# The opening of an attention and gated feed-forward kernel: its hand-written order through the fifth tile's step written anew, with copies as entries of their own, line sums moved to VectorE, and late query loads placed behind the weights

## The chip, the cores and the metric

One Trainium2 chip, one of its cores. The metric is the device time of one execution in microseconds (us). The kernel before takes 1026.68 us, the median of three runs (1026.49 to 1027.34). The profile is of one further execution.

## What is computed

Attention over keys that are 4x4 averages of an image, followed by a gated feed-forward layer, all in one launch.

```python
# q (4, 12288, 128), kv (4, 384, 32, 128), w_sr (128, 128)
kv_pool = kv.reshape(B, H//4, 4, W//4, 4, C).mean(axis=(2, 4))
k = v = kv_pool.reshape(B, -1, C) @ w_sr            # 768 keys per image
a = exp(s - max(s)),  s = (q @ k.T) / sqrt(C)
x = (a / a.sum(-1)) @ v                              # 49152 rows of 128
out = (relu(x @ w_gate) * (x @ w_val)) @ w_out       # d_ff = 1536
```

The kernel does not subtract the maximum and divides by the row sums only at the end, squared, since the gate and the value are both linear in x.

## The kernel before, in words

**Tiles.** The rows are cut into 96 tiles of 512. Per tile TensorE does 6 rows of score matmuls (keys in 6 chunks of 128), 6 value matmuls, and for each of 12 blocks of the hidden layer one value projection, one gate projection and one output projection. Tiles 0 to 3 are the lead: their attention is done with scores transposed (keys on partitions, `scores` and `lead_values`), and their row sums are made on TensorE with a block of ones (`lead_sums`, four tiles side by side in 32-column strips of the array).

**Order.** Every engine runs its instructions in the order in which the program lists them. That order is written out by hand. The string `OPENING` lists the work up to the first gate and value projections of tile 0; after it, the loop over `k` from 4 runs a list of words per step (`FIRST` for steps 4 and 5, then `STEADY`). Step `k` does the scores of tile k (`s0` to `s3`, exponentials `e0` to `e3`), the projections of tile k-3 (`v`, `y`, `g`, `h`) and the output of tile k-4 (`o`, closed by `oT`). Step 4 is the fifth tile's step, step 5 the sixth. `FIRST` begins `r v1 o0 v8 v10 o1 v4 s0`: in step 5, `o0` and `o1` are the output matmuls of tile 1 that read the gate products of hidden blocks 0 and 1.

**Words.** A word names a step and its numbers; `v1.2` is tile 1, hidden block 2, `S0.5` tile 0, key chunk 5.

- `a`, `b`, `c`, `p`, `r`: sums of image lines (128x512 float32), then of pixels, of one key chunk, on the engine that `ENGINES` names (`a` ScalarE, `v` VectorE, `p` GpSimd; VectorE if none). `SUMS` says which lines. A chunk has four lines; those not summed are summed by TensorE while it turns them.
- `T5.3`: TensorE turns line 3 of chunk 5, four 128x128 transposes that add in one bank (`turn_add`); `T3.p` two transposes, of the two pixel sums; `T2.r` one. `kvT` copies the turned chunk out, `pj` multiplies it by `w_sr`, `key` stores it as keys, `vt` and `val` make the values of it.
- `cast`, `qt`, `qT`: queries to 16 bits, turned, copied.
- `S`, `V`, `U`: score matmul, value matmul, sums with ones. `R`: inverts the row sums (VectorE). `xT`: copies a tile's attention result.
- `v`, `g`: value and gate projection; in the old opening each also issues the copy of its result (`keep_value`) or the gate product (`gated`). `y` is that copy, `h` that product (VectorE, reads the gate's bank and the copy).
- `gate`, `W0`, `W1`, `wo`: a one-column copy on GpSimd that waits for an image line, then the loads of the weights, issued by GpSimd. `gate22` waits for line 2 of chunk 5.

**Banks.** PSUM has eight banks of 128x512. `bank` takes the first free one in the order in which they were freed; two of the eight (6 and 7) are given up for a wide tile (`wide_ps`, scores of tiles from 4 on) when the opening ends.

**Loads.** The sync queue (SP) carries the lines of key chunks 0 and 1, then w_sr, queries and lines of chunks 2 and 3, four transfers of lines of chunks 4 and 5 (`kv_line`), each 512 KB, and then eight transfers of 64 KB for the queries of tiles 5 and 4 (`q_late`, line 173). DMA issues of SP and GpSimd wait on their own queues in listed order.

## Time and profile before

| what | us |
|---|---|
| median of three runs | 1026.68 |
| span of the profiled execution, first to last instruction | 1024.5 |
| TensorE busy in it | 1019.4 |
| ScalarE busy | 919.9 |
| VectorE busy | 861.8 |
| GpSimd busy | 524.8 |
| first transpose of an image line on TensorE starts at | 8.07 |
| first value projection (tile 0) starts at | 27.84 |
| step 5 starts at (its first value projection) | 45.71 |
| granted TensorE clock, mean | 1.000 |

Times inside the run are counted from the span's first instruction. The median is 2.2 us above the span of the profiled execution: start and end of an execution lie outside of the span. In a timeline row, the columns are start, duration of the merged stretch, engine, line, operation, what is written and read, shape and count, and in brackets the idle time before it with what ended it. On TensorE a matmul's row shows when it starts and a modelled end; the next one starts before that end.

## The change

The list `OPENING` is written anew and now runs through the whole of step 4: its scores (`s`, `e`), the projections of tile 1, and the output of tile 0 (`o`, `oT`) are mixed with those of tile 0, and the loop starts at step 5. The exponentials (`E`), the copies of value projections (`y`) and the gate products (`h`) are words of their own, each with its place in its engine's order. A word may name its bank after an `@`. Several outputs of one bank may now be added in any order of blocks (`o_left`, `sums_left`). `ENGINES` names VectorE for nearly all line sums (GpSimd keeps `a1`), for more copies of the opening, and for three of the 24 copies `y` of tiles 0 and 1 (1.11, 1.7, 1.9). Chunks 2 and 5 get line sums and a sum of pixels (`a`, `p`, `r`), and give up eight and eight transposes for one each. The ones matmuls go in six groups of four (`U0` to `U5`) in place of one of 20 and one of 4. The gate before the weights waits for line 1 of chunk 4 (`gate2.1`). The loads of the late queries become words (`ql4`, `ql5`) behind `W1`; a one-element memset on GpSimd into their tile goes ahead of them. The queries of tiles 6 and 7 are loaded in four words (`qd`), their transposing transfer (`tq1`) stands after `s0`.

```diff
     ENGINES = dict(word.split(":") for word in """
-        key0:a val0:a a1:p kvT1:a key1:a val1:a key2:a val2:a a3:p b3:p p3:p kvT3:a val3:a
-        cast0:a cast1:a qT1:a cast3:a cast4:p cast5:p xT1:a xT3:a
+        a1:p p1:v kvT1:a cast0:v cast1:v key1:a kvT0:v qT1:v qT0:a val1:v key0:a cast3:v cast2:v
+        val0:v qT3:a a2:v qT2:v p2:v a3:v r2:v b3:v c3:v kvT2:a p3:v key2:a kvT3:a val2:v a5:v
+        key3:v p5:v a4:v r5:v b4:v val3:a c4:v kvT5:a p4:v key5:v kvT4:v val5:a key4:v val4:v
+        cast4:p xT1:v xT2:v cast5:p y1.11:v y1.2:a xT3:v y1.4:a xT0:a y1.0:a y1.3:a y0.6:a y0.4:a
+        y0.5:a y0.3:a y0.11:a y0.1:a y1.8:a y0.0:a y0.8:a y1.7:v y0.2:a y1.10:a y0.9:a y0.7:a
+        y0.10:a y1.1:a y1.5:a y1.9:v y1.6:a
     """.split())
     OPENING = """
-        T0.1 T1.3 cast1 T0.3 cast0 T1.2 T0.2 a1 p1 T1.p T0.0 kvT1 kvT0 pj1 qt1 pj0 T2.0 qT1 a3
...
+        a1 p1 T1.p@0 T0.0@1 T1.3 T1.2 T0.2 kvT1 T0.1 cast0 pj1@0 cast1 T0.3 key1 qt1@2 kvT0 vt1@0
+        qt0@3 qT1 pj0@1 qT0 val1 S1.1@2 key0 S0.1@0 E1.1 vt0@1 S0.0@3 cast3 S1.0@4 E0.1 cast2
+        V1.1@2 qt3@5 E1.0 val0 V0.1@0 qt2@1 qT3 a2 V1.0 E0.0 S3.1@4 qT2 S3.0@5 E3.1 V0.0 p2
+        S2.1@1 E3.0 a3 T2.2@3 V3.1@4 E2.1 r2 V3.0 b3 S2.0@5 T2.r T2.3 E2.0 c3 V2.1@1 kvT2 U1@6
+        V2.0 pj2@3 p3 U0 key2 T3.p@5 S0.2@3 kvT3 vt2@7 S1.2@5 E0.2 val2 gate2.1 a5 pj3@7 W0 E1.2
+        S3.2@3 key3 V0.2 p5 E3.2 S2.2@5 S2.3@7 a4 E2.2 V1.2 W1 ql4 ql5 T5.2@3 E2.3 r5 vt3@5 V2.2
+        b4 T5.r val3 V3.2 T5.3 wo c4 S1.3@5 kvT5 V2.3 E1.3 S0.3@7 p4 pj5@3 E0.3 U2 key5 T4.p@5
+        V1.3 kvT4 vt5@3 S3.5@7 val5 V0.3 E3.5 S2.5@5 pj4@3 E2.5 S1.5@7 key4 V3.5 E1.5 vt4@3
+        S1.4@5 val4 V2.5 E1.4 cast4 S2.4@3 V1.5 E2.4 S3.4@7 qT4 V1.4 S3.3@5 E3.4 xT1 V2.4 S0.5@3
+        E3.3 qd1 V3.4 xT2 S0.4@7 E0.5 cast5 v1.11@2 V3.3 E0.4 y1.11 v1.2@5 qd3 g1.2@1 qT5 y1.2
+        v1.4@3 xT3 qd0 V0.4 V0.5 y1.4 g1.11@2 qd2 h1.2 g1.3@5 xT0 v1.0@4 g1.4@3 h1.11 y1.0 v1.3@1
+        v0.6@0 U3 h1.4 y1.3 v0.4@2 g0.6@4 y0.6 U4 h1.3 v0.5@1 y0.4 v0.3@3 h0.6 g0.4@0 y0.5 v0.1@5
+        v0.11@2 h0.4 y0.3 U5 g0.3@1 g0.5@4 y0.11 R o4@0 v1.8@3 y0.1 o6 h0.5 v0.0@2 y1.8 s0 h0.3
+        g0.1@5 y0.0 g1.8@3 tq1 v1.7@4 h0.1 e0 o3 v0.8@1 v0.2@2 h1.8 g0.8@5 y0.8 s1 y1.7 y0.2
+        g0.9@3 g0.2@1 o1 e1 h0.8 g0.11@2 v1.10@4 h0.2 o5 y1.10 v0.9@5 s2 h0.11 qn11 y0.9 o2
+        g0.0@1 e2 v0.10@4 v0.7@2 h0.9 g1.10@5 o8 y0.7 o11 h0.0 v1.1@3 y0.10 s3 h1.10 g0.10@1 y1.1
+        v1.5@2 g0.7@4 h0.10 e3 o0 v1.6@3 h0.7 v1.9@5 g1.7@1 y1.5 o10 y1.9 o9 y1.6 o7 g1.0@2 h1.7
+        g1.1@4 g1.9@3 g1.6@5 oT g1.5@1 h1.0 h1.9 h1.5 h1.6 h1.1
     """.split()
...
-    SUMS = [{}, {"a": [0, 1]}, {}, {"a": [0, 1], "b": ["s", 2], "c": ["s", 3]}, {"a": [0, 1], "b": ["s", 2], "c": ["s", 3]}, {}]
+    SUMS = [{}, {"a": [1, 0]}, {"a": [0, 1]}, {"a": [0, 1], "b": ["s", 2], "c": ["s", 3]}, {"a": [0, 1], "b": ["s", 2], "c": ["s", 3]}, {"a": [0, 1]}]
...
     def q_load_tile(i):
         q32 = work.tile([128, T], FP32, tag="o_t", bufs=2, name="q32_late")
+        nc.gpsimd.memset(q32[0:1, 0:1], 0.0)
...
     def lead_sums(chunks):
-        if "sums" not in x_banks:
-            x_banks["sums"] = bank([128, T])
         for jc in chunks:
+            first = "sums" not in x_banks
+            if first:
+                x_banks["sums"] = bank([128, T])
+            sums_left[0] -= 1
...
-    q_load_tile(5)
-    q_load_tile(4)
...
         elif head == "U":
-            lead_sums(range(at[0] * (NJC - 1), NJC - 1 + at[0]))
+            lead_sums(at)
...
         elif head == "v":
             value_proj(*at)
+        elif head == "y":
             keep_value(*at)
         elif head == "g":
             gate_proj(*at)
+        elif head == "h":
             gated(*at)
...
         elif head == "gate":
-            nc.gpsimd.tensor_copy(gate, line(at[0] // 4, at[0] % 4)[:, 0, 0:1])
+            nc.gpsimd.tensor_copy(gate, line(2 * at[0], at[1])[:, 0, 0:1])
+        elif head == "ql":
+            q_load_tile(at[0])
...
+        elif head == "o":
+            out_proj(0, at[0])
+            image_step(1, 0, at[0])
+        elif head == "oT":
+            out_moves.extend(out_turn(0))
+        elif head == "s":
...
+            score_block(LEAD, at[0])
+        elif head == "e":
+            exp_block(LEAD, at[0])
+            if at[0] % 2:
+                a_turn(LEAD, at[0] - 1, at[0] + 1)
...
-    for k in range(LEAD, last + 1):
+    for k in range(LEAD + 1, last + 1):
```

## What was predicted, before the result was known

> **What bounds the kernel now.** First the page's busy times, then the chain of waits, then TensorE's timeline around the change.

> ```profile
> PE 1019.4 (100%) x5048; PEld 489.5 (48%) x5048; DVE 861.8 (84%) x1432; ACT 919.9 (90%) x1931; POOL 524.8 (51%) x1308
> ...
> PE 98%; DMA 1%; ACT 1%; SPq 0%; issue 0%
> ```

> TensorE is busy throughout and the chain stays on it for 98%. From step 5 on its 512-column matmuls start 0.216 us apart, so the change can only alter when step 5 gets going. That is read from the opening.

> ```profile
> 22.27 0.66 PE L270 MATMUL bank_ps<-ident,kv_line 128*128 128x128 f32 x4
> ...
> 27.84 0.38 PE L455 MATMUL bank_ps<-xT,wv 128*128 128x512 f16 x1
> 28.06 0.38 PE L468 MATMUL bank_ps<-xT,wg 128*128 128x512 f16 x1
> 28.37 1.26 PE L432 MATMUL bank_ps<-aT,ones 128*32 128x512 f16 x20
> 29.56 0.39 PE L455 MATMUL bank_ps<-xT,wv 128*128 128x512 f16 x1
> ...
> 45.71 0.38 PE L455 MATMUL bank_ps<-xT,wv 128*128 128x512 f16 x1
> 45.93 0.38 PE L496 MATMUL bank_ps<-hT,wo 128*128 128x512 f16 x1
> 46.14 0.59 PE L455 MATMUL bank_ps<-xT,wv 128*128 128x512 f16 x2
> 46.57 0.38 PE L496 MATMUL bank_ps<-hT,wo 128*128 128x512 f16 x1
> ```

> T5.3, the last image line, starts at 22.27 (the weight load before it waited for the DMA). Step 5 begins at 45.71 and its second output matmul, o1 of tile 1, at 46.57: the point I compare. VectorE, which makes the gate products that this matmul reads:

> ```profile
> 29.23 0.69 DVE L476 SCALAR_TENSOR_TENSOR hT<-bank_ps,val 128x512 f16<-128x512 f32 x1
> 30.36 0.72 DVE L440 STREAM_TRANSPOSE sums_turned<-bank_ps 128x512 f32<-128x512 f32 x1 [0.44 <-PE bank_ps L432]
> ...
> 31.49 6.69 DVE L476 SCALAR_TENSOR_TENSOR hT<-bank_ps,val 128x512 f16<-128x512 f32 x11
> 38.65 0.69 DVE L462 CAST val<-bank_ps 128x512 f16<-128x512 f32 x1 [0.47 <-PE bank_ps L455]
> 39.26 7.42 DVE L476 SCALAR_TENSOR_TENSOR hT<-bank_ps,val 128x512 f16<-128x512 f32 x12
> 46.59 0.71 DVE L504 STREAM_TRANSPOSE o_t<-bank_ps 128x512 f32<-128x512 f32 x1
> ```

> From 29.23 to 47.30 VectorE has hardly a gap. TensorE is the bound on paper, but in this stretch VectorE runs level with it.

> **Part 1: TensorE's own work.** Turning line by line costs 0.11 us per transpose (four from 18.69 to the next matmul at 19.13). Chunks 2 and 5 fall from 16 transposes to nine each: 14 x 0.11 = -1.5. The ones matmuls use 32-column strips, and each switch to or from them costs time: 28.06 to 28.37 is 0.31 instead of 0.216, the way out 0.11 (29.88 to 30.21 for four that take 0.216). That is 0.2 per group; six groups instead of two add 0.8. [...]

> The new list has 48 transposes (5.3), 6 projections (1.3), 22 turns of queries and values (16 x 0.056 and 6 x 0.056: 1.2), 108 matmuls of 512 columns (23.3), 6 groups of ones (2.5) and 4 score pairs (0.324 each, 1.3): 34.9 us. It begins with T1.p, for which a1 on GpSimd (6.37 to 7.63) and p1 on VectorE (7.66 to 8.09) are needed: 8.25. Without a wait, step 5 would begin at 43.2 instead of 45.71.

> **Part 2: the line that lands last.** T5.3 cannot go before 22.27 (a little earlier perhaps, below). Behind it the list holds 83 matmuls of 512 columns (17.9), four groups of ones (1.7), the score pairs (1.3) and small ones (1.2): 22.1 us. So step 5 begins at 44.4 at the earliest, 1.3 ahead of before. Moving sums off TensorE buys nothing ahead of this line: TensorE then waits for it.

> **Part 3: sums and copies moved.** On VectorE a line sum takes 0.69, a pixel sum 0.42 (GpSimd's took 1.26 and 0.73). VectorE gains four of the larger kind (a2, a3, b3, a5), three pixel sums (p2, p3, p5) and two half ones (r2, r5): 4 x 0.69 + 3 x 0.42 + 2 x 0.25 = 4.5, before 23 us, and it was busy 4.5 of the 14 us from 8 to 22: hidden, unless T2.r or T5.r stand in front of TensorE; uncovered it would cost up to 4.5. T5.r needs a5, p5, r5 behind val2, key3 and a4 in VectorE's queue; lines 0 and 1 of that pair are there by 19.3 (the gate on line 2 fired at 20.60, pieces of 512 KB follow each other by 1.3: 12.89 to 14.21 in the first waits), so 19.8 + 0.69 + 0.3 + 0.4 + 0.69 + 0.25 = 22.1. It comes level with T5.3. I take T5.3 at 22.4 (22.2 to 22.6).

> **Part 4: ScalarE up to the first gate product.** Behind T5.3 the list has 11 of the 24 exponentials, paced 0.48 apart (the row of eight from 24.83 takes 4.05). The first follows T5.3 (0.44) and S1.3's 0.41: 23.25. Without waits the eleven and val5 (0.22) end at 28.8. Two waits: val5 stands ahead of E3.5 and needs vt5, which comes behind U2, T4.p and V1.3 on TensorE, at 24.7 (ScalarE idle 0.6); S1.5 is told to use bank 7, which E3.5 frees (0.2). So y1.2, queued behind E0.4, runs 29.6 to 30.2, and h1.2, the first product, starts at 30.2, where before it was 29.23. xT3 is put ahead of it on VectorE and ends at the same time. Bounds: 29.4 (no wait), 30.6 (T5.3 at 22.6, and a little in each hand-over).

> **Part 5: VectorE to the end of its list.** From h1.2 to the end of h1.1: 24 products at 0.60 (11 in 6.69), R 1.13 (30.36 to 31.49), y1.7 and y1.9 at 0.61, oT 0.7, the last one's tail 0.08: 17.5. Before, the same stretch had 24 products, R and one copy (16.1), and ended at 46.59 after 1.2 us of gaps. I take 1.0 of gaps (0.1 to 1.3): 30.2 + 17.5 + 1.0 = 48.7. **That is the step that decides:** the list ends `oT g1.5 h1.0 h1.9 h1.5 h1.6 h1.1`, and step 5 begins `v1 o0 v8 v10 o1`. o1 reads h1.1, now the last of all, with oT and four products ahead of it. Even if TensorE reached g1.5 on time, five products take 3.1 us from there, while o1 is due 1.1 us after it. The banks say the same: at g1.5 five of six hold gates that wait for VectorE. So o1 runs at 48.7 where it ran at 46.57: +2.1. Behind it waits all of step 5 on TensorE. VectorE and ScalarE catch up during the wait, so I expect nothing more to be late; the 0.27 at 55.3 (a score pair that waited for ScalarE) may go.

> **Part 6: loads.** The gate fires on line 1 of chunk 4, 1.3 earlier, at 19.3. The weights were there in time before (27.84 waited for none), so this is worth nothing on the path. The late queries are no longer issued from 12.89 on, but behind GpSimd's four weight issues (0.7, 0.6, 0.6, 0.6), from 21.9; eight at 0.31 end at 24.4. The median landing of `q_late` was 5.9 us, so tile 4's are there by 28 to 29; its cast (0.61) and transposing transfer (5.4) give 34 to 35. s0 comes at 35.9: some 1 us of cover. On GpSimd `wo`, both casts and the `qd` loads stand behind the memset, on SP qT4, qT5, tq1 and the first image lines behind the late queries; all have several us. Cost nothing; if the landing slips by 2 us, s0 waits 1.

> **Sum.** Own work and line: up to -1.3. VectorE's end, which replaces it: +2.1 (from 29.4 + 17.5 + 0.1 = 47.0, +0.4, to 30.6 + 17.5 + 1.3 = 49.4, +2.8). The span 1024.5 becomes 1026.6; the median stood 2.2 above the span: **1028.8**.

> **Rivals.**
> *VectorE keeps pace, TensorE decides (faster).* Needs h1.2 at 27.9 or earlier, since h1.1 must end by 45.4. For it: TensorE's list alone would be through at 44.4. Against: ScalarE's eleven exponentials after the last line. -1.3, 1025.4; up to -2.0 if that line lands 0.4 earlier without the late queries beside it and the 0.27 goes too. [...]
> *Level (no change).* First product at 29.4 to 29.8 and gaps of VectorE near 0.1: o1 at 47.0 to 47.6, +0.4 to +1.0, 1027.4. For it: VectorE's queue is full, so gaps may vanish. Against: 1.2 us of gaps before.
> *The weights delay the last line (slower).* The weights' first packets moved 1.9 us after their first issue (22.6 after 20.73; they landed 4.8 to 6 after it), so now at 21.3, with the last line still under way till 22.2. If they take half the engines from there, 0.9 us of line becomes 1.8, T5.3 and all behind it slips by 0.9: +3.0, 1029.7. It decides as soon as T5.3 slips beyond TensorE's own arrival at it, 22.5. [...]

> **How the numbers follow.** About 0.2% (2.05 us) is what a measurement of this kernel can tell from no change. VectorE's end decides with +1.0 to +2.8: 0.58, of it 0.40 above 2.05, since T5.3 and the hand-overs more likely add than save. Level 0.22. Weights or late queries in the way 0.12, all above. TensorE decides 0.08, half of it beyond 2.05. Faster 0.04, same 0.18 + 0.22 + 0.04 = 0.44, slower 0.52. The likeliest's own range is 1027.7 to 1029.5; with level, a late line (+3.0, and 0.9 for late queries on top) and part of the faster case, 1026.4 to 1030.8.

> **What would show it.** Right: the timeline of TensorE after: 48 image transposes, T5.3 near 22.4, h1.2 on VectorE near 30.2, the first gap of over 0.5 on TensorE just ahead of o1 in step 5, ended by VectorE's line 476. Wrong: h1.2 before 29.4, step 5 begun by 44.5 and o1 without a wait, or T5.3 past 22.8 with a DMA as its releaser, or s0 waiting for qT4.

## The result, and the profile after

The changed kernel takes 1029.59 us, the median of ten executions (1028.17 to 1034.42), against 1026.86 for ten of the kernel before beside it (1026.23 to 1027.35). The ratio is 1.0036 (1.0026 to 1.0047): slower, by a little more than what can be told from no change. The forecast was 1028.8. The medians alone stand at 1.0027; the ratio is larger because the long executions weigh in it. Of the ten, the five shortest (1028.17 to 1029.14) surround the forecast; the other five go from 1030.03 to 1034.42.

The profiled execution took 1030.03, its span is 1028.1 instead of 1024.5. From its page, the busy times and the chain of waits:

```profile
PE 1020.5 (99%) x5034; PEld 488.2 (47%) x5034; DVE 867.8 (84%) x1445; ACT 919.3 (89%) x1927; POOL 522.8 (51%) x1307
...
PE 98%; DVE 1%; DMA 1%; ACT 0%; issue 0%; POOL 0%; DVEq 0%; ACTq 0%; POOLq 0%
```

TensorE has 14 matmuls fewer and is still the chain; new on it is VectorE, with its line 499, the gate products (L499 in the rows below). Where that is shows in TensorE's timeline (start, length of the merged stretch, engine, line, operation, what is written and read, idle time before it and who ended that):

```profile
22.53 0.60 PE L284 MATMUL bank_ps<-ident,kv_line 128*128 128x128 f32 x4
...
44.72 0.81 PE L491 MATMUL bank_ps<-xT,wg 128*128 128x512 f16 x3
45.77 0.38 PE L477 MATMUL bank_ps<-xT,wv 128*128 128x512 f16 x1 [0.24 <-DVE o_t L529]
46.35 0.38 PE L521 MATMUL bank_ps<-hT,wo 128*128 128x512 f16 x1 [0.20 <-DVE hT L499]
46.95 0.38 PE L477 MATMUL bank_ps<-xT,wv 128*128 128x512 f16 x1 [0.22 <-DVE hT L499]
47.54 0.38 PE L477 MATMUL bank_ps<-xT,wv 128*128 128x512 f16 x1 [0.22 <-DVE hT L499]
48.74 0.38 PE L521 MATMUL bank_ps<-hT,wo 128*128 128x512 f16 x1 [0.82 <-DVE hT L499]
48.95 0.39 PE L477 MATMUL bank_ps<-xT,wv 128*128 128x512 f16 x1
49.17 0.82 PE L377 MATMUL wide_ps<-kv,qT 128*128 128x512 f16 x2
49.78 0.63 PE L477 MATMUL bank_ps<-xT,wv 128*128 128x512 f16 x1
...
52.34 0.73 PE L491 MATMUL bank_ps<-xT,wg 128*128 128x512 f16 x2
52.90 0.38 PE L477 MATMUL bank_ps<-xT,wv 128*128 128x512 f16 x1
```

T5.3 starts at 22.53. Step 5 begins at 45.77. Its first four matmuls wait for banks that VectorE frees one by one, and o1 runs at 48.74 instead of 46.57: 2.17 later. Then comes what no step of the prediction has: from 49.17 to 52.34 the matmuls start 0.43 apart. VectorE up to there:

```profile
30.45 3.13 DVE L499 SCALAR_TENSOR_TENSOR hT<-bank_ps,val 128x512 f16<-128x512 f32 x5
33.85 0.69 DVE L499 SCALAR_TENSOR_TENSOR hT<-bank_ps,val 128x512 f16<-128x512 f32 x1 [0.27 <-PE bank_ps L491]
34.56 0.72 DVE L462 STREAM_TRANSPOSE sums_turned<-bank_ps 128x512 f32<-128x512 f32 x1
...
44.42 0.68 DVE L499 SCALAR_TENSOR_TENSOR hT<-bank_ps,val 128x512 f16<-128x512 f32 x1
45.01 0.70 DVE L529 STREAM_TRANSPOSE o_t<-bank_ps 128x512 f32<-128x512 f32 x1
45.64 3.04 DVE L499 SCALAR_TENSOR_TENSOR hT<-bank_ps,val 128x512 f16<-128x512 f32 x5
```

The first gate product is at 30.45, the last ends at 48.68, with one gap of 0.27 between and no other above 0.11. The matmuls 0.43 apart are a matter of the clock. The table by stretches (length, busy time and count of PE, PEld, DVE, ACT, POOL, then the granted clock, the DMA engines' share, GB/s):

```profile
46.00:48.00 2.00, 1.28 (x4) 0.29 (x3) 2.00 (x4) 1.17 (x2) 2.00 (x4) 1.00 1.05 236
48.00:50.00 2.00, 1.26 (x5) 0.62 (x5) 0.69 (x2) 1.17 (x2) 2.00 (x4) 0.80 1.18 274
50.00:52.00 2.00, 2.00 (x6) 0.70 (x5) 1.32 (x3) 1.17 (x3) 0.66 (x2) 0.50 1.35 88
52.00:54.00 2.00, 2.00 (x10) 0.90 (x9) 1.77 (x4) 0.99 (x3) 0.55 (x1) 0.85 1.37 58
```

A mean of 0.80 over 2 us is 0.8 us at half clock, 0.85 is 0.6: with the 2 us between, 3.4 us at 0.5, right behind a stretch in which TensorE was busy for 1.28 and 1.26 of 2 us. From s0's first matmul to the tenth behind it takes 3.73 us (49.17 to 52.90); the same ten take 2.08 in a kernel where the clock stayed up (49.07 to 51.15 in `filled`, below). So the half clock costs 1.65. The last matmul of the kernel starts at 1024.65 instead of 1021.10: 3.55 later, of 2.17 + 1.65 = 3.82; the other 0.3 is made good somewhere behind o1.

## The experiments

All kernels are the changed one with one edit, save `before_loads`, which is the kernel before with one, and `combined`. The clean measure is the time from T5.3 to o1, since T5.3 moves with the landing of the last image line. "Line" is the time from the third line's landing to the last one's.

| kernel | line | T5.3 | o1 | T5.3 to o1 | span | median (executions) | ratio (interval) |
|---|---|---|---|---|---|---|---|
| before | 1.67 | 22.27 | 46.57 | 24.30 | 1024.5 | 1026.86 (10) | 1 |
| changed | 1.24 | 22.53 | 48.74 | 26.21 | 1028.1 | 1029.59 (10) | 1.0036 (1.0026 to 1.0047) |
| again | 2.76 | 23.14 | 49.41 | 26.27 | 1028.8 | 1029.81 (12) | 1.0031 (1.0015 to 1.0046) |
| relabel | 1.25 | 22.49 | 47.71 | 25.22 | 1025.9 | 1028.99 (12) | 1.0021 (1.0003 to 1.0039) |
| filled | 1.26 | 22.43 | 48.64 | 26.21 | 1026.5 | 1028.86 (12) | 1.0024 (1.0008 to 1.0039) |
| outputs_first | 1.25 | 22.39 | other place | | 1029.5 | 1030.95 (12) | 1.0036 (1.0019 to 1.0053) |
| ones_in_two | 1.23 | 22.62 | 48.75 | 26.13 | 1026.4 | 1029.38 (12) | 1.0035 (1.0022 to 1.0048) |
| copies_back | 2.81 | 23.32 | 49.58 | 26.26 | 1027.6 | 1031.72 (6) | 1.0059 (1.0040 to 1.0079) |
| one_copy | 2.83 | 23.37 | 49.19 | 25.82 | 1027.1 | 1029.22 (6) | 1.0032 (1.0020 to 1.0043) |
| short_scales | 1.28 | 22.40 | 48.28 | 25.88 | 1030.1 | 1032.18 (6) | 1.0050 (1.0032 to 1.0069) |
| loads_back | 1.78 | 22.63 | 48.84 | 26.21 | 1027.2 | 1029.24 (8) | 1.0025 (1.0016 to 1.0035) |
| before_loads | 1.24 | 22.20 | 46.45 | 24.25 | 1024.6 | 1026.35 (11) | 0.9998 (0.9989 to 1.0006) |
| queries_early | 1.25 | 22.58 | 48.79 | 26.21 | 1026.5 | 1028.99 (11) | 1.0022 (1.0014 to 1.0031) |
| combined | 1.72 | 23.09 | 47.86 | 24.77 | 1026.7 | 1028.05 (11) | 1.0012 (0.9998 to 1.0025) |

### Does the place of o1's product decide: relabel

Tile 1's hidden blocks are given other numbers, so that h1.0 and h1.1 are made first and the last five products are those of blocks 7 to 11. Work and order of every engine stay.

```diff
...
-        g1.1@4 g1.9@3 g1.6@5 oT g1.5@1 h1.0 h1.9 h1.5 h1.6 h1.1
+        g1.11@4 g1.8@3 g1.10@5 oT g1.9@1 h1.7 h1.8 h1.9 h1.10 h1.11
```

> The changed kernel with the hidden blocks of tile 1 renumbered in the opening, so that the last five gate products are blocks 7 to 11 and step 5's first output matmuls (o0, o1) read products made long before. Everything else stands in the same order. Theory (VectorE's list ends late, and o1 waits for its last entry): o1 at 47.8 instead of 48.74; the four short waits for banks ahead of it stay (they wait for the same five products), so step 5 gains about 0.9 and the span is 1025.5 to 1027.2 by whether TensorE's clock still drops. Rival (the banks alone hold step 5, the product that o1 reads does not matter): v4 and all behind it stay where they are, no gain.

TensorE's timeline:

```profile
45.73 0.38 PE L477 MATMUL bank_ps<-xT,wv 128*128 128x512 f16 x1 [0.24 <-DVE o_t L529]
46.30 0.38 PE L521 MATMUL bank_ps<-hT,wo 128*128 128x512 f16 x1 [0.20 <-DVE hT L499]
46.90 0.38 PE L477 MATMUL bank_ps<-xT,wv 128*128 128x512 f16 x1 [0.22 <-DVE hT L499]
47.50 0.38 PE L477 MATMUL bank_ps<-xT,wv 128*128 128x512 f16 x1 [0.22 <-DVE hT L499]
47.71 0.38 PE L521 MATMUL bank_ps<-hT,wo 128*128 128x512 f16 x1
```

o1 waits for no product any more and runs 1.0 earlier against T5.3; the four waits for banks before it are what they were, and even o0 (46.30), whose input is now long there, waits for VectorE: it opens a bank for its output, and none is free. The clock stays up and the span is 2.2 lower. So of the 1.9 between T5.3 and o1 that the change lost, 1.0 is the place of h1.1 at the end of the list; the other 0.9 goes with the four waits for banks, which stay.

### Does another order of step 5 avoid it: outputs_first

Step 5 lists its scores and the outputs whose products are ready first.

```diff
...
+        r s0 o2 o3 o4 o8 v1 e0 o10 o7 v8 y1 o11 o0 v10 y8 v4 y10 v5 g5 g10 v0 o9 y4 y5 h10 y0 g4
...
-        words = FIRST if kV < LEAD else STEADY if k < NT else DRAIN if k < last else LAST
+        words = FIRST5 if k == LEAD + 1 else FIRST if kV < LEAD else STEADY if k < NT else DRAIN if k < last else LAST
```

> The changed kernel with step 5 alone listed otherwise: s0 and six output matmuls of tile 1 whose products are long there come first, the value projections that need VectorE's banks between and behind them. Same work. Theory (VectorE is behind by some 3 us at the end of the new list, and step 5's order makes TensorE wait for it): waits in step 5 under 0.6 in all instead of 2.6, no drop of the clock, span 1024.3 to 1025.0, level with before. Rival (the loss lies in the opening itself, at the latest image line or the loads): still 2 us over before.

Missed: the waits in step 5 were 0.37, 0.25, 0.18, 0.34 and 0.61, together 1.75 us where under 0.6 was expected. VectorE still has the same work to do before step 5's projections find banks, so most of the waiting only changes places (the last wait is for ScalarE). The order does help a little: the shortest span of its executions is 1025.8, that of the changed kernel's 1026.4. The profiled execution was longer for another reason, which its timeline shows:

```profile
104.01 0.38 PE L482 MATMUL bank_ps<-xT,wv 128*128 128x512 f16 x1
106.44 0.39 PE L424 MATMUL bank_ps<-aT,kv 128*128 128x512 f16 x1 [2.06 <-DMA aT<-a]
106.67 0.43 PE L496 MATMUL bank_ps<-xT,wg 128*128 128x512 f16 x1
106.89 0.85 PE L382 MATMUL wide_ps<-kv,qT 128*128 128x512 f16 x2
107.53 0.63 PE L424 MATMUL bank_ps<-aT,kv 128*128 128x512 f16 x1
```

A value matmul waited 2.06 us for a transposing transfer of the scores (`aT<-a`), and after it the matmuls start 0.43 apart again.

### Is it the waiting that halves the clock: filled

Eight matmuls into an unused wide bank are listed into step 5's waits; nothing reads them.

```diff
...
+        r z1 v1 z1 o0 z1 v8 z1 v10 z4 o1 v4
```

> The changed kernel with eight extra matmuls of 512 columns into an unused wide bank in step 5: one ahead of each of v1, o0, v8, v10 and four ahead of o1. They compute nothing that is used, and take 1.7 us of TensorE time where it waits now. Theory (the granted clock fell to 0.5 for 3.4 us because TensorE paused 2.5 of the 3.3 us before): the clock stays at 1.0, no matmul of step 5 is 0.43 apart, o1 stays at 48.7 and the span is 1026.4 to 1026.7 in every run. Rival (the drop has nothing to do with the pauses): the clock drops as before, the span is 1028 or more in some runs.

```profile
46.00:48.00 2.00, 1.99 (x9) 0.67 (x7) 2.00 (x5) 1.26 (x3) 2.00 (x4) 1.00 1.10 252
48.00:50.00 2.00, 2.00 (x11) 0.88 (x9) 0.78 (x2) 1.23 (x3) 2.00 (x4) 1.00 1.12 266
50.00:52.00 2.00, 2.00 (x11) 0.96 (x10) 2.00 (x4) 1.57 (x4) 1.10 (x3) 1.00 1.36 158
```

In the same view as above, TensorE is busy throughout and the clock stays at 1.00. o1 runs at 48.64, as late as before the edit: the matmuls cover the waits and delay nothing. That alone doesn't settle the cause, since half clock doesn't follow the waits every time: of six profiles with the same five waits, `changed` and `again` show it, `queries_early`, `ones_in_two`, `loads_back` and `short_scales` don't.

What sets these apart can be sought in the trace's record of the granted clock. In `changed` it shows the full clock from 4.82 on, then 0.50 from 49.19, 44.37 us later, for 3.413 us, and the full clock again from 52.60. In `outputs_first` it shows the full clock from 4.47 on and the drop from 106.87, 102.40 later. The two distances are 13.0 and 30.0 times the 3.413 us for which the drop lasted in `changed`, so I compare stretches of that length, counted from the first full clock of each record. The stretch ahead of the drop and the drop itself in `changed`, then the stretch at the same count in `again`, `ones_in_two` and `queries_early`:

```profile
45.77:49.18 3.41, 1.95 (x7) 0.58 (x7) 2.92 (x5) 1.76 (x3) 3.38 (x6) 1.00 1.06 270
49.20:52.59 3.39, 3.39 (x10) 1.31 (x9) 1.91 (x3) 2.07 (x4) 1.49 (x4) 0.50 1.36 112
46.35:49.76 3.41, 1.85 (x6) 0.57 (x6) 3.01 (x6) 1.76 (x3) 3.28 (x6) 1.00 1.06 273
46.25:49.67 3.42, 2.05 (x8) 0.77 (x8) 2.44 (x5) 1.99 (x4) 3.34 (x7) 1.00 1.08 265
46.39:49.80 3.41, 2.14 (x9) 0.81 (x9) 2.35 (x4) 1.98 (x4) 3.41 (x7) 1.00 1.18 210
```

TensorE is busy for 1.95 and 1.85 us where half clock follows, for 2.05 and 2.14 where it doesn't (2.15 in `loads_back`, 2.16 in `short_scales`). In `filled` it is busy for 3.99 of the 4 us from 46 to 50, and the clock stays at 1.00. So half clock followed the waits in those executions in which TensorE was busy least in the stretch; that this is what decides is my reading of these profiles, no run shows it by itself. The busy times are modelled, and the figures are those of this place only.

The second half of the expectation, the span of 1026.4 to 1026.7 in every run, was missed: three of the twelve executions are above 1030.5, and two of these, above 1033, show a mean clock of 0.998, as one drop of 3.4 us gives. The half clock of step 5 isn't the only thing that makes executions long.

### How even is the result: again

> The changed kernel, unchanged, for a second profile. Its ten runs lie between 1028.2 and 1034.4, those of before within 1.1. Theory (pause plus clock): the same waits to 0.1 us up to o1 at 48.7, and a span of 1026.4 to 1028.1 by where in time the clock's drop falls, with one or more runs above 1030 whose cause is open. Rival (a load lands late in some runs): o1 past 49.5 with a DMA ahead of it.

The changed kernel once more, unedited. TensorE's timeline at T5.3:

```profile
22.05 0.38 PE L436 MATMUL bank_ps<-aT,kv 128*128 128x512 f16 x1
23.14 0.66 PE L284 MATMUL bank_ps<-ident,kv_line 128*128 128x128 f32 x4 [0.71 <-DMA kv_line<-in_kv_dram]
```

Here the last line landed 2.76 us after the third (`changed`: 1.24), TensorE waited for it, and all up to o1 comes 0.6 to 0.7 later, at 49.41. The five waits are the same; the span of 1028.8 lies above the expected range, and a DMA came late ahead of o1, nearly as in the rival. In three of the eleven profiles with the changed loads the line took 2.76 to 2.83, in the other eight 1.23 to 1.28; with the loads as before it took 1.67 to 1.78 in three profiles.

The sign is that of the third rival, but not its way of coming about. The DMA queues from 21.4 to 22.6 (packets, MB, share of 16 engines; q0 carries the weights, q1 the image lines), first in `changed`, then in `again`:

```profile
q0 software_dynamic: 129, 0.19, 92.4%
q8 instruction: 1, 0.02, 3.3%
...
q0 software_dynamic: 154, 0.21, 102.7%
q1 hardware_dynamic: 2, 0.00, 2.4%
q8 instruction: 1, 0.02, 3.4%
```

The weights are under way in both, and nearly all of the line is there by 21.4; in `changed` no packet of q1 is left. What is late in `again` is the line's last packet of 4 KB and a short packet behind it (4 bytes in `changed`). The packet of 4 KB starts at 22.00, and the single packet of 16 KB of the queue `instruction` runs from 20.94 to 22.01. In `copies_back` the two times are 22.14 and 22.15; in `one_copy` only the short packet is late, at 22.26, and the packet of 16 KB ends at 22.28. So in these three executions the late packet started within 0.02 us of that packet's end, while the rest of the line had landed; that the one held up the other is inferred from these times and not shown. In the other eight profiles with the changed loads the packet of 16 KB begins at 20.7 to 21.2 too, and the line isn't late; in the kernel before it begins at 22.23, behind the line.

### VectorE's copies: copies_back and one_copy

```diff
-        y0.10:a y1.1:a y1.5:a y1.9:v y1.6:a
+        y0.10:a y1.1:a y1.5:a y1.9:a y1.6:a
```

That is `one_copy`; `copies_back` gives y1.7 to ScalarE too.

> The changed kernel with the copies y1.7 and y1.9 on ScalarE instead of VectorE; same work. Theory (VectorE's list sets when o1 runs): VectorE has 1.2 us less ahead of h1.1, o1 at 47.5 to 47.7 instead of 48.74, span of the fastest runs 1025.3 or less. Rival (ScalarE is as full as VectorE there and takes the 1.2 back): o1 unmoved within 0.3, span unmoved.

> The changed kernel with the copy y1.9 alone back on ScalarE (43.8 in the changed kernel's profile, where ScalarE has 1.5 us idle from 44.6 on). With both copies back ScalarE, full around 38, held up the products. Theory (VectorE's end sets o1, and the copy at 43.8 is cover that ScalarE has): o1 at 48.1 to 48.3 instead of 48.74 with T5.3 at 22.5, span 0.5 lower than with the same clock before, 1025.9 to 1026.7 without the half clock, median 1028.3 to 1029.0. Rival (ScalarE is the one that sets the end): o1 unmoved at 48.6 to 48.8.

With both copies the theory missed: from T5.3 to o1 it takes 26.26, unmoved, though VectorE has 1.2 us less to do. The rival was right, as TensorE's timeline in `copies_back` shows:

```profile
40.19 0.38 PE L491 MATMUL bank_ps<-xT,wg 128*128 128x512 f16 x1 [0.32 <-ACT val L485]
...
46.47 0.81 PE L491 MATMUL bank_ps<-xT,wg 128*128 128x512 f16 x3 [0.28 <-ACT val L485]
```

ScalarE now frees the banks too late. With y1.9 alone, which falls into time that ScalarE has (1.53 us idle before 46.19 in the changed kernel), it takes 25.82: 0.39 less, of 0.6 taken from VectorE. Its o1 is at 49.19 because the line came late; with T5.3 at 22.5 it would be at 48.3, as expected. The median, 1029.22, is above the expected 1028.3 to 1029.0.

### VectorE's work itself: short_scales

```diff
...
-        nc.vector.transpose(turned.rearrange("p x m -> p (x m)"), freed(x_banks.pop("sums")))
+        nc.vector.transpose(turned[:, 0], freed(x_banks.pop("sums"))[:, 0:32])
...
```

> The changed kernel with R cut short: of the row sums only the first 32 columns are turned and inverted, so the scales of tiles 0 to 3 are not those of the reference. VectorE does 0.7 to 0.8 us less between 34.6 and 35.7. Theory (from R to the end of h1.1 VectorE has no gap and its end sets o1): o1 at 48.0 to 48.1 with T5.3 at 22.5, 0.6 to 0.7 earlier, and TensorE's waits ahead of o1 smaller by about that much together. Rival (TensorE's order or ScalarE's copies set the products' times): o1 at 48.5 or later, and VectorE shows new gaps of 0.5 us together between 35 and 48.

R, from its transpose to the next product, took 0.60 (34.43 to 35.03) where it took 1.13 (34.56 to 35.69): 0.53 less, not 0.7 to 0.8. From T5.3 to o1 it takes 25.88, 0.33 less. So VectorE's work does reach o1, though over a third of what is taken away is lost again; o1 at 48.28 lies between the two theories. The expectation had the wrong place for the gain: the five waits ahead of o1 are what they were (0.41, 0.36, 0.38, 0.38, 0.98), and what goes is an earlier wait of 0.31 on TensorE, at 37.02 in the changed kernel. The execution's length comes from elsewhere: a wait of 2.25 us at 107.24 for the same transfer as in `outputs_first`, with half clock behind it.

### TensorE's own work: ones_in_two

```diff
...
-        v0.6@0 U3 h1.4 y1.3 v0.4@2 g0.6@4 y0.6 U4 h1.3 v0.5@1 y0.4 v0.3@3 h0.6 g0.4@0 y0.5 v0.1@5
+        v0.6@0 h1.4 y1.3 v0.4@2 g0.6@4 y0.6 h1.3 v0.5@1 y0.4 v0.3@3 h0.6 g0.4@0 y0.5 v0.1@5
-        v0.11@2 h0.4 y0.3 U5 g0.3@1 g0.5@4 y0.11 R o4@0 v1.8@3 y0.1 o6 h0.5 v0.0@2 y1.8 s0 h0.3
+        v0.11@2 h0.4 y0.3 U2.3.4.5 g0.3@1 g0.5@4 y0.11 R o4@0 v1.8@3 y0.1 o6 h0.5 v0.0@2 y1.8 s0 h0.3
```

> The changed kernel with the ones matmuls in two groups (8 and 16) instead of six of four. Same matmuls, four switches to strips and back less: 0.8 us of TensorE's own time by the 0.2 per group of the trace. Theory (TensorE waits for VectorE at the end, so its own work does not count): o1 within 0.4 of 48.7, and no gain beyond 0.4. Rival (TensorE's own work decides): 0.8 faster.

The ones matmuls in two groups instead of six leave o1 where it was, as expected: 26.13 from T5.3. TensorE's own work behind the last line doesn't set o1.

### The loads: loads_back and before_loads

`loads_back` gives the changed kernel the late queries and the weights' gate as before; `before_loads` gives the kernel before those of the change. From `before_loads`:

```diff
-        V1.1 S2.0 b3 c3 S2.1 S3.0 S3.1 T2.2 V0.1 T2.3 V1.0 kvT2 V2.1 V0.0 p3 gate22 W0 W1 cast4
+        V1.1 S2.0 b3 c3 S2.1 S3.0 S3.1 T2.2 V0.1 T2.3 V1.0 kvT2 V2.1 V0.0 p3 gate17 W0 W1 ql4 ql5 cast4
...
```

> The changed kernel with the loads as before the change: late queries issued from SP behind the image lines without GpSimd's memset, weights held on line 2 instead of line 1 of the last pair. Theory (the loads cost nothing where the last line lands on time, but in some runs the weights share the engines with it: it landed 1.24 after the third line in one profile of the changed kernel and 2.76 after it in another): the last line lands 1.6 to 1.7 after the third as before the change, T5.3 starts at 22.3 to 22.6, and the fastest runs stay within 0.4 of the changed kernel's. Rival (the loads are the loss): the span falls by 1 or more.

> The kernel before with the change's loads alone: the weights held on line 1 of chunk 4, the late queries issued by SP behind W1, the memset on GpSimd ahead of them. Theory (the loads are not what costs the +2.1, and a late last line comes in some executions): median 1026.7 to 1027.5, in most executions the span of before, T5.3 0.2 to 0.4 earlier (the last line's landing 1.2 to 1.3 after the third) or, where the weights come beside that line, up to 1 us later. Rival (the loads cost something in each execution): 1027.6 or more.

Neither moves the time from T5.3 to o1 (26.21 and 24.25). By themselves the new loads cost nothing: 0.9998, and the eleven executions lie between 1026.09 and 1026.65. T5.3 came only 0.07 earlier although the line landed at 21.74, because TensorE itself got there at 22.20; the expected 0.2 to 0.4 was wrong for that reason.

### The pile-up behind step 4: queries_early

The query loads of tiles 8 to 11 (`qn`, GpSimd) are let go by h0.4 instead of h0.11.

```diff
-        v0.11@2 h0.4 y0.3 U5 g0.3@1 g0.5@4 y0.11 R o4@0 v1.8@3 y0.1 o6 h0.5 v0.0@2 y1.8 s0 h0.3
+        v0.11@2 h0.4 qn4 y0.3 U5 g0.3@1 g0.5@4 y0.11 R o4@0 v1.8@3 y0.1 o6 h0.5 v0.0@2 y1.8 s0 h0.3
...
-        g0.9@3 g0.2@1 o1 e1 h0.8 g0.11@2 v1.10@4 h0.2 o5 y1.10 v0.9@5 s2 h0.11 qn11 y0.9 o2
+        g0.9@3 g0.2@1 o1 e1 h0.8 g0.11@2 v1.10@4 h0.2 o5 y1.10 v0.9@5 s2 h0.11 y0.9 o2
```

> The changed kernel with one word moved: the load of the queries of tiles 8 to 11 waits for tile 0's product 4 (done at 34.6) instead of product 11 (40.9), so GpSimd issues it some 6 us earlier, about where it was before the change (37.1). Same work. Theory (the slow runs come from transposing transfers of tile 4 and later that land late, since these query loads and the first image lines now go out beside them: issued at 43.7, landed 61.1 in the changed kernel, 46.2 and 50.2 before): tile 4's second transfer lands by 52, the transfers of tiles 8 to 14 land 5 us or more ahead of their first value matmul again, at most one run in ten above 1030.5, fastest runs as in the changed kernel. Rival (the slow runs come from elsewhere): a quarter or more of the runs above 1030.5 as before this edit.

The issues of DMAs in the window of tile 4's second transposing transfer (count, size, us from issue to landing), first in the changed kernel:

```profile
q<-in_q_dram POOLq DMA_DIRECT2D x1, 128.0 KB, 9.4
aT<-a SPq DMA_TRANSPOSE x1, 17.4
```

In the kernel before:

```profile
aT<-a SPq DMA_TRANSPOSE x1, 4.0
```

In queries_early:

```profile
aT<-a SPq DMA_TRANSPOSE x1, 6.8
```

In the changed kernel the transfer, issued at 43.7, runs beside the query loads issued from 41.2 on and lands at 61.1. Those were issued at 37.1 before the change, and are at 35.2 here. The delay is not over with tile 4: over tiles 4 to 14 the second transfer landed 1.0 to 8.9 us ahead of the matmul that reads it, 4.6 to 11.5 before the change, 7.4 to 13.3 in `queries_early`, and 0.0 at the two waits of over 2 us seen above. The times of the other executions go along with it: above 1030.5 were 35 of 96 executions of the changed kernel and its variants that keep the late load, 1 of 22 of the two with the early one, 5 of 94 of the kernel before. Three of those 35 were profiled. `outputs_first` and `short_scales` (1032.25 and 1032.91) show the wait for `aT<-a`; `again` (1030.61) doesn't, its length is the late line and the half clock in step 5. So the early load takes nearly all long executions away, which is shown; that each of them had this wait is likely, not shown.

### The parts together: combined

`relabel`, `queries_early`, the loads of `loads_back` and the copy of `one_copy` in one kernel.

> The changed kernel with tile 1's blocks renumbered, the group-2 query load at h0.4 instead of h0.11, the late queries and the weights' gate as before, and the copy ahead of the last but two of tile 1's values (y1.9, now called y1.8) on ScalarE. Theory: the parts add: o1 at 47.0 to 47.3 (47.71 with the numbers alone, 0.6 less for the copy), no half clock, span 1025.0 to 1025.6, median 1027.2 to 1027.9, few or no executions above 1030.5, so 0.3 to 1.1 above before: level, not faster, since VectorE is still through with the list's products later than the kernel before. Rival (something of the order still waits for the banks): span 1025.9 or more, 1028.0 or more.

From T5.3 to o1 it takes 24.77, 0.5 more than before: the parts add. With T5.3 at 22.5, o1 would be at 47.3, as expected; it is at 47.86, and the span of 1026.7 is over the expected 1025.6. T5.3 was late (23.09) because the whole list began 0.5 later: T1.p at 8.84 instead of 8.31, behind warm-up matmuls that ended later. None of its eleven executions is above 1029.72. The median, 1028.05, is 1.3 above the 1026.75 of the kernel before beside it and just misses the 1027.9 expected. It is faster than the change, and not faster than the kernel before, which no version found beats.

## Why the prediction came out as it did

The direction, the place and the size of the decisive step were right, and the median lies 0.8 above the forecast. By its own steps:

- **Part 1.** T1.p at 8.31 for 8.25. The groups of ones don't matter for o1 (`ones_in_two`), as Part 2's argument, that TensorE only waits longer, has it.
- **Part 2 and 3.** T5.3 at 22.53 for 22.4; the line had landed 0.7 earlier, so it was TensorE's own arrival (the "22.5" of the third rival). No turn waited for VectorE's line sums: hidden.
- **Part 4.** The first gate product at 30.45 for 30.2, inside its bounds.
- **Part 5, "the step that decides".** o1 at 48.74 for 48.7. That it agrees to 0.04 is luck, for two errors cancel: the start was 0.25 late, and the stretch took 18.2 instead of 18.5. Counted as in the forecast, 18.2 less 17.5 of work, 0.7 of the 1.0 of gaps was there: the one of 0.27, pauses of 0.11 and less, and the overlap of instructions lost around them. `relabel` shows that both halves of the reason hold, the place of h1.1 (1.0 us) and the banks (four waits, which stay without it). What the step left out is ScalarE: two copies given back to it undo nothing (`copies_back`), so VectorE and ScalarE share the bound.
- **"VectorE and ScalarE catch up during the wait, so I expect nothing more to be late"** is the step that failed. True of the two engines, it left out two things. One is what came behind the wait on TensorE itself: half clock for 3.4 us, which cost 1.65 us in the profiled execution, most of the difference between 1026.6, the span forecast, and 1028.1. Where the clock stays up (`queries_early`, `ones_in_two`) the span is 1026.4 to 1026.5, the forecast's. The other is a load, below. Both are needed for the median: the five shortest of the ten executions have a mean clock of 1.000 and spans of 1026.4 to 1027.3, about as forecast. Of the five above 1030, three have 0.998 and two have 1.000, so the half clock doesn't explain all of them.
- **Part 6.** s0 ran at 35.74 without a wait, as said, and the loads cost nothing on the path by themselves (`before_loads`). It looked at the loads that the change moves and not at those that move along with the gate products: `qn` waits for h0.11 and is issued 4 us later than before. By the counts of `queries_early` and `combined` that makes most of the long executions.
- **The rivals.** A late last line happens, in three of eleven profiles, by 0.6 to 0.8 instead of 0.9, on top of VectorE's end and not in its place. The half share of the engines, on which the third rival's +3.0 is reckoned, is shown by no run: the weights' first packets moved at 20.9 in `changed` and at 20.7 in `again`, and the line landed 1.24 and 2.76 us after the third. Late was only a last packet of the line, which started when a packet of 16 KB of another queue ended (22.00 and 22.01 in `again`). "TensorE decides" and "Level" are excluded by the five waits, in the fence above, that VectorE ends.

## What to carry to other kernels

## What the runs showed of the hardware

**Half clock followed short pauses, in some executions.** The five pauses ahead of o1 are 0.41, 0.36, 0.38, 0.38 and 0.98 us over the usual distance of 0.216, together 2.5 us within 3.4 us; none is long by itself. The clock then stood at 0.50 for 3.4 us in two of six profiles (from 49.19 in `changed`, from 49.76 in `again`), and there was half clock after the single waits of 2.06 us (`outputs_first`) and 2.25 us (`short_scales`) too. In `changed` and `outputs_first` the drop begins 44.37 and 102.40 us behind the first full clock in the trace's record, 13.0 and 30.0 times the 3.413 us for which the drop lasted in `changed`. In the stretch of that length ahead of the drop TensorE was busy for 1.95 us in `changed` and 1.85 in `again`; in the stretch at the same count it was busy for 2.05 to 2.16 in the four profiles without a drop in step 5. That stretch lies elsewhere against the same waits in each execution: it begins at 45.77 in `changed`, at 46.66 in `loads_back`. With matmuls in the pauses (`filled`) the clock stood at 1.00 from 44 to 54. What lowers the clock is not shown beyond this.

**A transposing transfer took longer with other loads beside it.** Tile 4's second transfer of scores took 4.0 us from issue to landing before, and 17.4 with eight query loads of 128 KB on GpSimd's queue and the next image lines around it, while the DMA engines moved only 58 to 88 GB/s at a share above 1.3 (50 to 54 us in the table of stretches). In all ten profiles with the late query load it took 14.4 to 18.3, in the two with the early one 5.0 and 6.8.
